# Down projection: the product with the lower left weight block as seven products over both column halves

## The chip, the cores and the metric

The kernel runs on one core of a Trainium2 chip. The metric is the device time of one execution in microseconds, the median of three runs. Most numbers below come from one further execution that the hardware profiler recorded.

## The reference

```
xn = _layernorm(x)                                   # x: 1 x 2048 x 640, float32
a = einsum("bsd,ed->bse", xn, dft_hid_re);  b = einsum("bsd,ed->bse", xn, dft_hid_im)
fnet = einsum("ts,bse->bte", dft_seq_re, a) - einsum("ts,bse->bte", dft_seq_im, b)
gate = einsum("bsd,df->bsf", xn, W_gate);  up = einsum("bsd,df->bsf", xn, W_up)     # f: 1728
h = gate * (gate > 0) * up
out = x + fnet + einsum("bsf,fd->bsd", h, W_down)
```

## The kernel before

**Arithmetic.** A product in float32 is made of three matmuls in the reduced type fp32r (`mm3`, lines 128 to 133): both operands are split (line 124) into a high copy, which ScalarE writes (line 125), and a low part, source minus high copy, which VectorE writes (line 126). The three matmuls are high by high, high by low and low by high.

**Stages.** First the Fourier transform over the sequence, to about 398 us; then gate and up, 26 units of one row block of the hidden layer each, to about 731 us; then the down projection, in which this change lies. It adds three things: the layernorm's transform still to be multiplied by the hidden DFT matrix ("hid", operands in `pqd`), the hidden activations times `W_down` ("f", operands in `hd`), and x itself (`xt`). The output is 640 rows (five row blocks e = 0 to 4 of 128) by 2048 tokens. The tokens are worked in two halves, q = 1 and then q = 0 (`project(q)`, line 1123), and each half is two chunks of 512 columns.

**The seven products.** The contraction blocks of 128 are paired, one "upper" and one "lower". Upper and lower blocks by the two column chunks, and the row blocks 0,1 against 2,3 of the output, make a 2 by 2 block product, and it is done with seven products in place of eight (Strassen's scheme in Winograd's form), named B11, T1, B21, T2, B22, T3 and T4. B11, B12 (used in T1), B21 and B22 are also the names of the four blocks of the moving operand: the first figure says upper (1) or lower (2) contraction blocks, the second says which column chunk. T1 to T4 use sums and differences of them, which VectorE makes. Row block e = 4 is done plainly, as a third column of weights beside B11, T1, B21 and B22. B21 is the product of the lower blocks of the first column chunk with the "lower left" weight block: each of its contraction blocks costs nine matmuls (row blocks 0, 1 and 4, three matmuls each).

**Units.** Each product is made of seven units, numbered 0 to 6: three "hid" units of two, two and one pairs of contraction blocks, an "f" unit of two, the "odd" unit 4 with the left-over rows (short in B21, B22 and T4), and two more "f" units of two. A unit of two blocks has 18 matmuls in B11, T1, B21 and B22 and 12 in T2, T3 and T4. The results gather in PSUM; after the last unit of a product VectorE adds them into an output tile `y` (`add_y`, line 1284) that was loaded with x.

**Order of the work.** All units stand in a list `todo`, in the order B11, T1, B21, T2, the first four units of B22, T3, the rest of B22, T4, for q = 1 and then for q = 0. `drive(4, 2)` walks it: at step i it issues the loads of unit i, prepares unit i-2 (the sums, the high copies on ScalarE, the low parts on VectorE), runs unit i-4 on TensorE and reads what ended with unit i-5. SyncE issues nearly all loads, strictly in this order; VectorE and ScalarE are ordered by a scheduler that a helper `in_turn` keeps near the program's order. Buffers come from pools: `raws` (24 tiles, "rw") for the moving operands as loaded, "ro" for the odd ones, `wraw` (4, "wr") and `wts` (5, "wt") for weights as loaded and as split, `ring2` (3, "cb") for the split moving operand. The weights' sums for T1, T2, T3, T4 and B22 are made once, during gate and up (`pair_weights`, line 1019), and stored to a DRAM array `wparts`.

Of the kernel before, what the change touches and what calls it, by code (L numbers as in the profile page):

```python
# [12 lines left out]
P = 128  # L13
S, D, F = 2048, 640, 1728
KD = D // P
CH = 512
# [41 lines left out]

@with_exitstack
def fnet_reglu_kernel(  # L60
# [40 lines left out]
    wparts = dram_p.tile([P, NPAIR, NW], F32, name="wparts")  # L101
    nc.vector.memset(eps_t, EPS)
# [915 lines left out]

    def pair_weights(k, n):

        t = {}

        def load():
            t["z"] = z = pool("prep").tile([P, Y12 + 2 * P], F32, name="pw")
# [6 lines left out]
        def prepare():  # L1031
# [15 lines left out]
        issues[n + 1].append(lambda: nc.gpsimd.dma_start(wparts[:, k], t["z"][:, :NW]))  # L1047
# [33 lines left out]
    def place(i):  # L1081
        if i % 2 == 0:
            spare[i // 2] = pool("prep").tile([P, Y12 + 2 * P], F32, name="pw")
        return spare[i // 2][:, i % 2 * W2 : (i % 2 + 1) * W2]
# [6 lines left out]
    for k in range(NPAIR):  # L1091
        pair_weights(k, 7 if k == ODD else 13 + k)
# [27 lines left out]
    for n, b, side in (("wraw", 4, "left"), ("ring2", 3, "left"), ("wts", 5, "left"), ("raws", 24, "left"), ("odd", 4, "right"), ("y", 1, "right")):  # L1120
        open_pools[n] = ctx.enter_context(tc.tile_pool(name=n, bufs=b, side=side, reuse_waits="tile"))

    def project(q):
        c0, c1 = 2 * q, 2 * q + 1
        units = [("hid", u) for u in HID_UNITS] + [("f", u) for u in F_UNITS]
        units.insert(ODD_AT, ("odd", (0,)))
        raws, B, y, ends = {}, {}, {}, []

        def get(kind, u):
            what, ks = units[u]  # L1130
# [16 lines left out]
        def unit(name, u, first):  # L1147
            what, ks = units[u]
# [7 lines left out]
            def load():  # L1156
                kind = {"T1": "B12"}.get(name, name)
                if name == "B11" and (q, u) == (1, 0):
                    return
                if kind in ("B11", "B12", "B21"):  # L1160
# [78 lines left out]
            def run():  # L1239
                b, w = t["b"], t["w"]  # L1240
                key, o, row4 = {"B11": ("a", 0, (2 * P, "v1")), "T1": ("b", P, (0, "v2")), "B21": ("c", 0, (2 * P, "v1")),
# [3 lines left out]
                for out, oo, more in [((key, i), o + i * P, more) for i in range(2)] + ([(row4[1], row4[0], name in ("B21", "B22"))] if row4 else []):  # L1245
                    if first and not more:
                        B[out] = bank()
# [118 lines left out]
```

## Time and profile before

| | |
|---|---|
| median of three runs | 1026.95 us (1026.6 to 1027.21) |
| the profiled execution: its span | 1025.6 us |
| PE (TensorE matmul) busy | 1019.3 us, 99%, 4525 matmuls |
| DVE (VectorE) busy | 805.5 us, 79%, 1113 instructions |
| ACT (ScalarE) busy | 448.2 us, 44% |
| moved by DMA | 236.45 MB, 231 GB/s in the mean |
| down projection on PE | 730.9 to 1021.5 us |

The profiled execution's time is its span and what lies around it; here only the span is recorded, 1025.6 us, which is 1.35 us under the median of the timed runs. In the profile's views PE is the matmul part of TensorE and PEld its weight load; `out<-in` names the tiles; "x6" counts instructions; a bracket at a row's end tells how long the engine idled before the row and what it waited for. The granted clock is the share of TensorE's full clock that it was given.

### The profile page before, as it was taken

Reading aid. Unit: us, or ns where it says so; the run is one execution under the profiler, and the core shown is the slowest. Engines: PE = TensorE matmul, PEld = TensorE weight load, DVE = VectorE, ACT = ScalarE, POOL = GpSimd, SP = SyncE. Lnnn points to the kernel's source line nnn. Section 1 sums busy time; section 2 is a strip of 40 time slices with the busy share of each in tenths; the row PEclk is TensorE's granted clock in tenths of the full one; section 3 lists DMA queues with packets and bytes.
Section 4 is the critical chain, followed back from the end, with each engine's and each line's share of the span. In section 5 each row is a group of like instructions: output and inputs, shape, how many; then the busy total and the mean of one; then the engine's idle time right before and its main releaser. Section 6 shows DMA issues by size and latency. Waiting matters only on the chain.

```text
span 1025.6 us, 12560 instructions
## 1 busy us (share of the span) xinstructions
PE 1019.3 (99%) x4525; PEld 843.1 (82%) x4525; DVE 805.5 (79%) x1113; ACT 448.2 (44%) x571; POOL 96.9 (9%) x161
## 2 busy tenths in 40 slices
PE   9999999999999999999999999999999999999998
PEld 7888888888888888888888888888888888888886
DVE  7967976969888797787887888876586779777776
ACT  6664453333334443433335544443454434553442
POOL 2000010121110001421110000000000001000000
PEclk9999999999999999999999999999999999999999
DMA  9884744976869665863474666664595747994655
GB/s 327 321 283 157 264 152 138 338 246 208 350 205 336 228 197 196 265 229 135 172 242 146 224 216 226 236 226 170 198 357 188 254 145 237 385 337 140 218 172 160
DMA packets 104542, 236.45 MB, mean 231 GB/s; under 512 B 11936, under 2 KB 55328, under 8 KB 102944
## 3 DMA queue, kind: packets, MB, share of 16 engines
q1 hardware_dynamic: 86896, 165.49, 47.9%
q0 software_dynamic: 17152, 69.74, 18.9%
q8 instruction: 35, 0.57, 0.2%
q10 hardware_dynamic: 432, 0.43, 0.1%
q14 instruction: 27, 0.22, 0.1%
HBM read 179.50 MB, written 55.07 MB: 229 GB/s over the span
## 4 chain that ended last, share of the span: by engine, by line
PE 97%; DVE 2%; DMA 0%; ACT 0%; issue 0%; SPq 0%; ACTq 0%
PE ps L132 31%; PE ps L131 31%; PE ps L133 31%; PE ps L519 3%; PE ps L548 1%; PE ps L1250 1%; DVE cb L126 1%; DMA raw<-in_dft 0%; DVE raw L686 0%; DVE r L126 0%; DVE sb L561 0%; DVE sa L558 0%; DVE tk L686 0%; ACT cb L125 0%; ACT cb L349 0%
## 5 line engine op out<-in xcount | busy, mean ns | idle before, releaser
L133 PE MATMUL ps<-cb,wt 128*128 128x512 f32 x412 | 160.0, 388 | 0.0
L132 PE MATMUL ps<-cb,wt 128*128 128x512 f32 x412 | 159.9, 388 | 0.0
L131 PE MATMUL ps<-cb,wt 128*128 128x512 f32 x412 | 159.8, 388 | 0.0
L125 ACT ACTIVATE cb<-rw 128x1024 fp32r<-128x1024 f32 x83 | 81.9, 987 | 121.7 <-PE ps L133 105.8
L126 DVE TENSOR_TENSOR cb<-rw,cb 128x1024 fp32r<-128x1024 f32 x83 | 94.0, 1132 | 50.9 <-ACT cb L125 50.5
L125 ACT ACTIVATE cb<-raw 128x1024 fp32r<-128x1024 f32 x64 | 67.8, 1060 | 103.7 <-PE ps L133 94.8
L126 DVE TENSOR_TENSOR cb<-raw,cb 128x1024 fp32r<-128x1024 f32 x64 | 78.2, 1221 | 31.9 <-ACT cb L125 31.6
L131 PE MATMUL ps<-xs_early,gw 128*128 128x512 f32 x260 | 101.1, 389 | 0.0
L132 PE MATMUL ps<-xs_early,gw 128*128 128x512 f32 x260 | 101.1, 389 | 0.0
L133 PE MATMUL ps<-xs_early,gw 128*128 128x512 f32 x260 | 101.1, 389 | 0.0
L133 PEld LDWEIGHTS ps<-cb,wt 128*128 128x128 f32 x412 | 77.3, 188 | 16.1 <-DVE wt L126 0.3
L131 PEld LDWEIGHTS ps<-cb,wt 128*128 128x128 f32 x412 | 77.3, 188 | 16.1
L132 PE MATMUL ps<-cb,xs_late 128*128 128x512 f32 x232 | 90.5, 390 | 0.1
L132 PEld LDWEIGHTS ps<-cb,wt 128*128 128x128 f32 x412 | 77.3, 188 | 15.9
L131 PE MATMUL ps<-cb,xs_late 128*128 128x512 f32 x232 | 90.3, 389 | 0.0
L133 PE MATMUL ps<-cb,xs_late 128*128 128x512 f32 x232 | 90.3, 389 | 0.0
L132 PE MATMUL ps<-cb,xs_early 128*128 128x512 f32 x226 | 87.9, 389 | 0.0
L131 PE MATMUL ps<-cb,xs_early 128*128 128x512 f32 x226 | 87.9, 389 | 0.0
L133 PE MATMUL ps<-cb,xs_early 128*128 128x512 f32 x226 | 87.9, 389 | 0.0
L122 ACT ACTIVATE gw<-z 128x1024 fp32r<-128x1024 f32 (+1 forms) x52 | 56.1, 1109 | 41.3 <-PE ps L133 29.4
L122 ACT ACTIVATE u<-ps 128x512 f32<-128x512 f32 x52 | 31.2, 599 | 89.6 <-PE ps L133 77.8
L867 DVE TENSOR_TENSOR gw<-z,gw 128x1024 fp32r<-128x1024 f32 (+1 forms) x52 | 64.8, 1284 | 2.9 <-ACT gw L122 2.8
(200 smaller groups left out, 1955.8 us busy)
## 6 DMA issues: line engine op xcount, KB each, us to landing
raw<-in_dft SPq DMA_DIRECT2D x94, 512.0 KB, 5.7
wt<-wparts SPq DMA_DIRECT2D x70, 256.0 KB, 3.2
z<-in_wgu SPq DMA_DIRECT2D x26, 640.0 KB, 4.6
hd<-ob POOLq DMA_DIRECT2D x26, 512.0 KB, 3.7
wparts<-pw POOLq DMA_DIRECT2D x12, 1024.0 KB, 4.1
rw<-hd SPq DMA_DIRECT2D x24, 512.0 KB, 5.9
tk<-in_dft SPq DMA_DIRECT2D x16, 512.0 KB, 8.1
rw<-pq SPq DMA_DIRECT2D x16, 512.0 KB, 6.3
```

Source lines behind the costliest of these rows:

```text
L122: return nc.scalar.activation(o, i, AF.Copy)
L125: nc.scalar.activation(hi, src, AF.Copy)
L126: return nc.vector.tensor_tensor(lo, src, hi.bitcast(F32), op=OP.subtract)
L131: nc.tensor.matmul(ps, wh, mh, start=first, stop=False, skip_group_check=more)
L132: nc.tensor.matmul(ps, wh, ml, start=False, stop=False, skip_group_check=more)
L133: nc.tensor.matmul(ps, wl, mh, start=False, stop=last, skip_group_check=more)
L519: nc.tensor.matmul(E[0, key], xn_part(n * SG + j, d)[v == 1], b[:, int(v == 2), j], start=False, stop=n % NH == NH - 1 and (j, v) == (SG - ...
L548: nc.tensor.matmul(E[c, key], xn_part(j, d)[v == 1], b[c][0][:, int(v == 2), j], start=j == 0 and v == 0, stop=False)
L867: tt(self.w[:, 1, cs], self.z[:, cs], self.w[:, 0, cs].bitcast(F32), op=OP.subtract)
L1250: nc.tensor.matmul(B[out], w[:, v, oo : oo + P], b, start=False, stop=u == len(units) - 1 and v == 1, skip_group_check=more)
```

## The change

The product B21 of both token halves, q = 1 and q = 0, has the same weights. Of its contraction blocks the ten full pairs that units 0, 1, 3, 5 and 6 hold are taken out of `project` and done for both halves at once, by a second level of the seven-product scheme (`second_level`): its two column halves are the first chunks of q = 1 (X) and of q = 0 (Y), its two contraction halves are pairs of blocks (QUADS), its two output halves are row blocks 0 and 1. The seven products are named 1, 2, 5, 6, 3, 7 and 4, and each goes over three groups of 2, 2 and 1 pairs of blocks, which makes 21 units. Row block 4 is again done plainly, beside products 1, 2, 5 and 3. Of B21 in `project` only units 2 and 4 (SINGLE) are left.

The operands X and Y are loaded once, by six DMAs into tiles of a new pool `quads` that stay on chip until the end (`fetch`); the output tiles of row blocks 0, 1 and 4 of both first chunks stay on chip too. These loads stand at step 14 of the list (LOADS_AT). The 21 units are put between the others, one after every second step (EVERY) from step 20 on (SINCE), that is from T2 of q = 1 to T1 of q = 0. The sums of weights that they need are made beside the others in `pair_weights` (four sums of 128 columns and a split of 512 for each of five quads) and stored to a new DRAM array `wquads`.

Other things move with it: the moving operands of B21 are still needed for T4, and are now loaded by T3's steps; those of B22's first units are loaded at T1 in place of B21; `raws` has 20 tiles in place of 24; the PSUM banks are named by hand; T4's first two units stand ahead of the left-over units of B21; and the order on TensorE follows the list too. `order` counts 4510 matmuls in place of 4525, and on VectorE 996 and 106 instructions of its two kinds of sums in place of 941 and 96.

```diff
+QUAD_LOW, QUAD_HIGH, NPREP = 16 * P, 20 * P, 24 * P
+QUADS = ((0, 2), (1, 3), (KD, KD + 2), (KD + 1, KD + 3), (KD + 4, KD + 5))
+GROUPS = (("hid", 0, 2, 0), ("f", 0, 2, 2), ("f", 4, 1, 4))
+PREP_ORDER = (0, 2, 1, 3, 4, 5, 7, 6, 8, 9, 10)
...
+        quad = next((i for i, (_, second) in enumerate(QUADS) if second == k), None)
...
+            if quad is not None:
+                halves = [[w[:, Y12 + i * P : Y12 + (i + 1) * P] for i in range(2)] for w in (made[QUADS[quad][0]], z)]
+                (a11, a21), (a12, a22) = halves
+                s1, s2, s3, s4 = (z[:, QUAD_LOW + i * P : QUAD_LOW + (i + 1) * P] for i in range(4))
+                minus = lambda o, i0, i1: nc.vector.scalar_tensor_tensor(o, i0, -1.0, i1, op0=OP.mult, op1=OP.subtract)
+                tt(s1, a22, a21, op=OP.subtract)
+                minus(s2, s1, a11)
+                tt(s3, a11, a21, op=OP.subtract)
+                minus(s4, a12, s2)
+                low = z[:, QUAD_LOW:QUAD_HIGH]
+                split(z[:, QUAD_HIGH:NPREP].bitcast(F32R), low, low)
...
+        def keep():
+            z = t["z"]
+            nc.gpsimd.dma_start(wparts[:, k], z[:, :NW])
+            if quad is not None:
+                for v, at in enumerate((QUAD_HIGH, QUAD_LOW)):
+                    nc.gpsimd.dma_start(wquads[:, quad, :, v], z[:, at : at + 4 * P].rearrange("p (s n) -> p s n", s=4))
...
+    pair_weights(ODD, 7)
+    for i, k in enumerate(PREP_ORDER):
+        pair_weights(k, 13 + i)
...
-    for n, b, side in (("wraw", 4, "left"), ("ring2", 3, "left"), ("wts", 5, "left"), ("raws", 24, "left"), ("odd", 4, "right"), ("y", 1, "right")):
+    for n, b, side in (("wraw", 4, "left"), ("ring2", 3, "left"), ("wts", 5, "left"), ("raws", 20, "left"),
+                       ("odd", 4, "right"), ("y", 1, "right"), ("quads", 1, "right")):
...
+    SINGLE = (2, ODD_AT)
+    LOADS_AT, SINCE, EVERY = 14, 20, 2
+    every = range(len(UNITS))
+    fixed = [bank() for _ in range(8)]
...
+        A, Bk = (fixed[0:2], fixed[2:4]) if q else (fixed[2:4], fixed[0:2])
+        B = {("a", 0): A[0], ("a", 1): A[1], ("b", 0): Bk[0], ("b", 1): Bk[1], ("c", 0): Bk[0], ("c", 1): Bk[1],
+             "v1": fixed[4], "v2": fixed[4], "v3": fixed[4]}
...
+                kind = {"B11": "B11", "T1": "B12", "T3": "B21"}.get(name)
+                if kind:
                     get(kind, u)
-
-                ahead = {("B21", 2): 0, ("B21", 4): 1, ("B21", 6): 2, ("T2", 0): 3, ("T2", 2): 4, ("T2", 3): 5, ("T2", 4): 6}.get((name, u))
+                ahead = {("T1", 2): 0, ("T1", 4): 1, ("T1", 6): 2, ("T2", 0): 3, ("T2", 2): 4, ("T2", 3): 5, ("T2", 4): 6}.get((name, u))
...
+        LOADS_Y = {"B11": ((0, 0), (1, 0), (4, 1), (4, 0)) if q else ((4, 1),), "T1": ((2, 1), (3, 1)), "T2": ((0, 1), (1, 1)), "T4": ((2, 0), (3, 0))}
...
+        steps = []
+        for name, us in (("B11", every), ("T1", every), ("T2", every), ("B22", every[:4]), ("T3", every),
+                         ("B22", every[4:]), ("T4", every[:2]), ("B21", SINGLE), ("T4", every[2:])):
+            whole = SINGLE if name == "B21" else every
...
+    def second_level():
+        X, Y = {}, {}
+        a, x, v = fixed[5:]
+        def fetch(g):
+            what, k, n, _ = GROUPS[g]
+            for t, q in ((X, 1), (Y, 0)):
+                t[g] = o = pool("quads").tile([P, 2 * n, CH], F32, name=f"q{q}{g}")
+                if what == "hid":
+                    nc.sync.dma_start(o, pqd[2 * q][1][:, k : k + 2 * n])
+                else:
+                    first = 2 * k + 1
+                    nc.sync.dma_start(o, hd[q][first : first + 4 * n - 1 : 2, :, :CH].rearrange("f p t -> p f t"))
+        def unit(name, g):
+            what, k, n, at = GROUPS[g]
+            k += KD if what == "f" else 0
+            t = {}
+            halves = slice(0, n), slice(n, 2 * n)
+            part = {"5": 0, "6": 1, "7": 2, "3": 3}.get(name)
+            second = name in ("2", "3", "4")
+            block = {"1": 0, "2": 0, "4": P}.get(name)
+            odd = name in ("1", "2", "5", "3")
+            def load():
+                own = pair(k + n * second, n)[1].rearrange("k p n -> p k n")
+                t["w"] = w = pool("wts").tile([P, 2, 2, 3 * P], F32R, name="wt")[:, :n]
+                if part is not None:
+                    for j in range(n):
+                        nc.sync.dma_start(w[:, j, :, :P].bitcast(F32), wquads[:, at + j, part])
+                if block is not None or odd:
+                    t["r"] = r = pool("wraw").tile([P, 2, 3 * P], F32, name="wr")[:, :n]
+                    if block is not None:
+                        nc.sync.dma_start(r[:, :, :P], own[:, :, block : block + P])
+                    if odd:
+                        nc.sync.dma_start(r[:, :, P : 2 * P], own[:, :, 2 * P : 3 * P])
+            def prepare():
+                lo, hi = halves
+                plus = lambda o, i: nc.vector.tensor_tensor(o, o, i, op=OP.add)
+                with in_turn():
+                    src = {"1": X[g][:, lo], "2": X[g][:, hi], "5": X[g][:, lo], "6": X[g][:, lo], "3": Y[g][:, hi],
+                           "7": Y[g][:, lo], "4": X[g][:, lo]}[name]
+                    if name in "5674":
+                        plus(src, {"5": Y[g][:, lo], "6": Y[g][:, hi], "7": Y[g][:, hi], "4": X[g][:, hi]}[name])
+                    t["b"] = b = pool("ring2").tile([P, 2, SG, CH], F32R, name="cb")[:, :, :n]
+                    lows.append(split(b[:, 0], b[:, 1], src))
+                    if "r" in t:
+                        cs = slice(0 if block is not None else P, 2 * P if odd else P)
+                        split(t["w"][:, :, 0, cs], t["w"][:, :, 1, cs], t["r"][:, :, cs])
+            def run():
+                b, w = t["b"], t["w"]
+                main, fresh = {"1": (a, True), "2": (x, True), "5": (x, True), "6": (a, False), "3": (x, False),
+                               "7": (a, False), "4": (a, False)}[name]
+                for ps, o, new in [(main, 0, fresh)] + ([(v, P, name in ("1", "5"))] if odd else []):
+                    for j in range(n):
+                        mm3(ps, (w[:, j, 0, o : o + P], w[:, j, 1, o : o + P]), (b[:, 0, j], b[:, 1, j]),
+                            new and g == 0 and j == 0, g == len(GROUPS) - 1 and j == n - 1, not new)
+            def read():
+                less = OP.subtract
+                for q, e, ps, op in {"1": ((1, 0, a, OP.add), (0, 4, v, less)), "2": ((1, 0, x, OP.add), (1, 4, v, OP.add)),
+                                     "5": ((0, 1, x, less),), "6": ((0, 0, a, less),), "3": ((0, 0, x, less), (0, 4, v, OP.add)),
+                                     "7": ((0, 1, a, less),), "4": ((1, 1, a, OP.add),)}[name]:
+                    add_y(q, e, 0, ps, op=op)
+            return load, prepare, run, read if g == len(GROUPS) - 1 else idle
...
+        loads = [((lambda g: lambda: fetch(g))(g), idle, idle, idle) for g in range(len(GROUPS))]
+        loads.append((lambda: get_y(0, (0, 0), (1, 0), (4, 0)), idle, idle, idle))
+        return loads, [unit(name, g) for name in "1256374" for g in range(len(GROUPS))]
+    def spread(steps, more, since, every_n):
+        mixed, more = [], list(more)
+        for i, s in enumerate(steps):
+            mixed.append(s)
+            if i >= since and (i - since) % every_n == every_n - 1 and more:
+                mixed.append(more.pop(0))
+        assert not more, len(more)
+        return mixed
+    steps = project(1) + project(0)
+    loads, quads = second_level()
+    steps[LOADS_AT:LOADS_AT] = loads
+    todo.extend(spread(steps, quads, SINCE, EVERY))
+    with tc.manual_schedule(engines={mybir.EngineType.SP, mybir.EngineType.Pool, mybir.EngineType.PE}):
```

Three places where instructions move follow. The names are the tiles with their numbers, so that `rw_6073` is a moving operand, `wr` weights as loaded, `q10` to `q02` the tiles of X (first figure 1) and Y (0), and `y000` an output tile of q = 0.

SyncE's queue of loads before, at T1 of q = 1: the loads of the odd unit 4 and of unit 5 (`rw_5959`).

```order
L1141 DMA ro_5936<-hd1_91 128x512
L1190 DMA wr_5938<-in_wd 128x128
L1191 DMA wr_5938<-wparts_94 128x256
L1145 DMA rw_5959<-hd1_91 128x2x512
L1190 DMA wr_5961<-in_wd 128x2x128
L1191 DMA wr_5961<-wparts_94 128x2x256
```

The same place now: between unit 4's weights and unit 5's operand (`rw_6073`) stand the nine loads of the change.

```order
L1260 DMA wr_5991<-in_wd 128x128
L1261 DMA wr_5991<-wparts_94 128x256
L1384 DMA q10_6012<-pq2_88 128x2048
L1384 DMA q00_6014<-pq0_86 128x2048
L1387 DMA q11_6032<-hd1_91 128x4x512
L1387 DMA q01_6034<-hd0_90 128x4x512
L1387 DMA q12_6054<-hd1_91 128x2x512
L1387 DMA q02_6056<-hd0_90 128x2x512
L1174 DMA y000_6058<-in_xt 128x512
L1174 DMA y100_6060<-in_xt 128x512
L1174 DMA y400_6062<-in_xt 128x512
L1216 DMA rw_6073<-hd1_91 128x2x512
```

Six transfers of four or two blocks of 128 x 512 and three output tiles now stand ahead of unit 5's operand.

VectorE before, near the end, at T4 of q = 0 (from the low part of its unit 2 on):

```order
L126 TENSOR_TENSOR cb_7858<-rw_7191,cb_7858 128x512
L1197 TENSOR_TENSOR ro_7279<-ro_7279,ro_7087 64x512
L1197 TENSOR_TENSOR rw_7304<-rw_7304,rw_7110 128x1024
L126 TENSOR_TENSOR cb_7884<-rw_7221,cb_7884 128x1024
L126 TENSOR_TENSOR wt_7915<-wr_7887,wt_7915 64x256 x2
L1197 TENSOR_TENSOR rw_7325<-rw_7325,rw_7131 128x1024
L1197 TENSOR_TENSOR cb_7912<-ro_7279,cb_7912 64x512
L126 TENSOR_TENSOR cb_7936<-rw_7304,cb_7936 128x1024
L126 TENSOR_TENSOR cb_7940<-rw_7325,cb_7940 128x1024
```

The same place now:

```order
L133 TENSOR_TENSOR cb_8014<-rw_7722,cb_8014 128x512
L1267 TENSOR_TENSOR rw_7786<-rw_7786,rw_7393 128x1024
L1179 TENSOR_TENSOR y000_6058<-ps_5723,y000_6058 128x512
L133 TENSOR_TENSOR cb_8031<-rw_7739,cb_8031 128x1024
L1179 TENSOR_TENSOR y100_6060<-ps_5724,y100_6060 128x512
L1179 TENSOR_TENSOR y400_6062<-ps_5727,y400_6062 128x512
L1267 TENSOR_TENSOR cb_8059<-ro_7766,cb_8059 64x512
L133 TENSOR_TENSOR wt_8062<-wr_8034,wt_8062 64x256 x2
L133 TENSOR_TENSOR cb_8083<-rw_7786,cb_8083 128x1024
L1267 TENSOR_TENSOR rw_7807<-rw_7807,rw_7416 128x1024
L133 TENSOR_TENSOR cb_8087<-rw_7807,cb_8087 128x1024
```

The three reads of the left-over B21 product (`y000`, `y100`, `y400`) have come in between, and the difference for the last unit (`rw_7807`) is made later, after the low part of the unit ahead of it.

More of the change, by code (lines that the diff above doesn't have):

```diff
@@ L1082, in place @@
         if i % 2 == 0:
[L1083 removed]
+            spare[i // 2] = pool("prep").tile([P, NPREP], F32, name="pw")
         return spare[i // 2][:, i % 2 * W2 : (i % 2 + 1) * W2]
@@ new lines, in fnet_reglu_kernel, with get_y, add_y @@
+    missing[0, 3, 0] += 2
+    def get_y(q, *which):
+        for e, c in which:
+            own = f"{q}" if e in (0, 1, 4) and c == 0 else ""
+            y[q, e, c] = t = pool("y").tile([P, CH], F32, name=f"y{e}{c}{own}")
+            nc.sync.dma_start(t, xt[e * P : (e + 1) * P, (2 * q + c) * CH : (2 * q + c + 1) * CH])
+    def add_y(q, e, c, ps, late=False, op=OP.add, at=slice(0, CH), queue=None):
+        t = y[q, e, c][:, at]
+        if op == OP.add:
+            nc.vector.tensor_tensor(t, ps, t, op=OP.add)
+        else:
+            nc.vector.tensor_tensor(t, t, ps, op=op)
+        missing[q, e, c] -= 1
+        if missing[q, e, c] == 0 or queue is not None:
+            first = (2 * q + c) * CH
+            o = out[e * P : (e + 1) * P, first + at.start : first + at.stop]
+            if queue is not None:
+                queue.dma_start(o, t)
+            elif late:
+                nc.sync.dma_start(o, t)
+            else:
+                defer(1, lambda: nc.gpsimd.dma_start(o, t))
```

119 lines of the change are left out of this document (51 added, 68 removed).

## The prediction

> **What bounds the kernel now.** I read the engines' busy times first, then the chain that ended last, then a table by windows of the down projection, and last the timeline of VectorE (DVE) and the DMA queue where the change puts work.
>
> ```profile
> PE 1019.3 (99%) x4525; PEld 843.1 (82%) x4525; DVE 805.5 (79%) x1113; ACT 448.2 (44%) x571; POOL 96.9 (9%) x161
> PE 97%; DVE 2%; DMA 0%; ACT 0%; issue 0%; SPq 0%; ACTq 0%
> 731.00:1021.50 290.50, 290.48 (x1287) 240.30 (x1285) 223.66 (x253) 131.67 (x163) 9.24 (x17) 1.00 0.72 241
> 876.49 0.19 PEld L133 LDWEIGHTS ps<-cb,wt 128*128 128x128 f32 x1 [0.30 <-DVE wt L126]
> ```
>
> TensorE (PE) is busy 99% of the span and carries 97% of the chain. The third row is the down projection (window; busy time and count of PE, PEld, DVE, ACT, POOL; granted clock; DMA share; GB/s): PE has no gap, the granted clock is 1.00. The last row is its only stall worth naming, 0.30 us. So a matmul taken out is gained in full, and every wait put in front of PE is lost in full, as nothing else has slack to give back. VectorE is busy 223.7 of 290.5 us there, 77%.
>
> ```profile
> 794.33 1.36 PE ps L1250 x6
> ```
>
> On the chain six matmuls take 1.36 us, 226.7 ns each.
>
> **The change part by part.** *Matmuls.* Ten blocks of B21 cost 9 matmuls each in two halves, 180. Now five quads cost 3 matmuls in each of 7 products, plus 4 times 3 for row block 4: 5 x 33 = 165. That is 15 fewer, 15 x 226.7 ns = -3.4 us, all on the path. The Trainium skill ("TensorE: Matmul & The Clock Gate", section "Wait — 56ns, not 53.3ns?") prices a matmul of 512 columns at about 216 ns; by it the term would be -3.2 us. The measured row decides.
>
> *Weights' sums in gate and up.* Five of the 26 units get four sums of 128 columns and a split of 512.
>
> ```profile
> 708.76 0.69 DVE L951 TENSOR_TENSOR oa<-ps,u 128x512 f32<-128x512 f32 x1 [1.73 <-PE ps L133]
> 701.26 0.42 DVE L856 TENSOR_TENSOR z<-z 128x256 f32<-128x256 f32 x1
> 701.60 0.28 DVE L857 TENSOR_TENSOR z<-z 128x128 f32<-128x128 f32 x1
> 701.80 0.68 DVE L878 TENSOR_TENSOR ob<-ob,u 128x512 f32<-128x512 f32 x1
> ```
>
> From start to start a 256-wide one takes 0.34 us and a 128-wide one 0.20 us; the split takes 0.605 (below): 4 x 0.20 + 0.605 = 1.4 us. The bracket shows VectorE idle for 1.73 us in such a unit, waiting for PE. I cost this at nothing; without that cover it would be at most 5 x 1.4 = 7 us.
>
> *VectorE's work in the down projection.* It runs its rows back to back where it is dense:
>
> ```profile
> 751.65 1.22 DVE L126 TENSOR_TENSOR cb<-rw,cb 128x1024 fp32r<-128x1024 f32 x1
> 752.79 0.95 DVE L126 TENSOR_TENSOR wt<-wr,wt 128x768 fp32r<-128x768 f32 x1
> 753.66 1.22 DVE L126 TENSOR_TENSOR cb<-rw,cb 128x1024 fp32r<-128x1024 f32 x1
> 754.79 0.69 DVE L1197 TENSOR_TENSOR rw<-rw 128x512 f32<-128x512 f32 x1
> 755.40 0.55 DVE L126 TENSOR_TENSOR wt<-wr,wt 128x384 fp32r<-128x384 f32 x1
> 755.87 0.68 DVE L1284 TENSOR_TENSOR y<-ps,y 128x512 f32<-128x512 f32 x1
> 756.47 0.68 DVE L126 TENSOR_TENSOR cb<-rw,cb 128x512 fp32r<-128x512 f32 x1
> ```
>
> From start to start: 1.135 us for 1024 columns, 0.87 for 768, 0.605 for 512, 0.47 for 384. The 21 new units need 14 low parts of 1024 and 7 of 512 (20.1 us), sums for four products, 8 of 1024 and 4 of 512 (11.5), and the lows of their weights (two products of 2 x 512 + 256, three of 2 x 256 + 128: 5.7), 37.3 us. Twelve more reads of PSUM add 7.3. Gone are ten units of B21, 1.135 + 0.87 each, 20.1. Net +24.5 us: VectorE goes from 223.7 to about 248 of 287 us, 86%. On the mean it fits. What counts is where it doesn't, and where its inputs come late. I find three places.
>
> *Place E, the loads at T1 of q = 1.* The queue of loads now has, ahead of unit 5's operand, six transfers for X and Y (5120 KB), three output tiles (768 KB), two of B22's operands that were loaded with B21 before (1024 KB) and one more output tile (256 KB): 7168 KB, 7.34 MB. Before:
>
> ```profile
> 735.00:757.50 22.50, 22.50 (x101) 18.63 (x100) 17.22 (x21) 11.27 (x15) 0.00 (x0) 1.00 1.01 364
> 740.00:750.00 10.00, 10.00 (x46) 8.28 (x45) 6.33 (x7) 4.52 (x6) 0.00 (x0) 1.00 1.05 390
> 10.00:12.00 2.00, 2.00 (x10) 1.68 (x9) 1.90 (x6) 0.83 (x4) 1.24 (x2) 1.00 1.02 423
> 752.11 0.38 SPq L1145 DMA_DIRECT2D rw<-hd  x1
> rw<-hd SPq DMA_DIRECT2D x1, 512.0 KB, 5.1
> 771.73 0.39 PE L131 MATMUL ps<-cb,wt 128*128 128x512 f32 x1
> 771.96 0.39 PE L132 MATMUL ps<-cb,wt 128*128 128x512 f32 x1
> 772.18 0.39 PE L133 MATMUL ps<-cb,wt 128*128 128x512 f32 x1
> 771.93 1.06 ACT L125 ACTIVATE cb<-rw 128x1024 fp32r<-128x1024 f32 x1 [0.25 <-PE ps L133]
> ```
>
> The first two rows show DMA full (share 1.01 and 1.05) through this stretch, moving 364 to 390 GB/s; the fastest I find elsewhere is 423. Unit 5's operand is issued at 752.11 and lands 5.1 us later, at 757.2, and the queue is full: what is put ahead of it moves it by its own length. At 390 GB/s 7.34 MB take 18.8 us, so it lands at 776.0 (774.6 at 423, 777.4 at 364). Then come the difference (1.135), the high copy (1.06) and the low part (1.135), and after them the second matmul, at 779.3; PE would have come to it at 771.96. That is 7.4 us, and up to 8.0 at the third matmul, whose weights' low part stands behind the operand's on VectorE. Nothing can pass: VectorE, ScalarE and PE each take their rows in order, and behind the waiting difference stand the low parts of units 5 and 6 and of T2. I take +8.0, with bounds 6 (at 423) and 9.4 (at 364); it would be 0 if the landing came by 768.6. The Trainium skill ("DMA: Bandwidth & Descriptors", section "Specifications") gives about 358 GB/s as a core's share of HBM; by it 20.5 us and a wait of 9.7. The window of 390 speaks against so low a limit here.
>
> A pause that long may also cost clock.
>
> ```profile
> 1022.50:1023.50 1.00, 0.00 (x0) 0.00 (x0) 0.00 (x0) 0.00 (x0) 0.00 (x0) 1.00 0.70 216
> 1023.50:1024.50 1.00, 0.00 (x0) 0.00 (x0) 0.00 (x0) 0.00 (x0) 0.00 (x0) 0.98 0.00 0
> 1024.50:1025.60 1.10, 0.00 (x0) 0.00 (x0) 0.00 (x0) 0.00 (x0) 0.00 (x0) 0.50 0.00 0
> 1.06 4.12 PE L113 MATMUL ps<-warm 128*128 128x128 bf16 x47 [1.06 <-DVE warm L109]
> 4.00:6.00 2.00, 1.18 (x22) 1.00 (x18) 1.85 (x8) 1.31 (x4) 0.00 (x0) 1.00 0.90 248
> ```
>
> PE stops at 1021.5, and the granted clock falls to 0.50 at about 1024.46, 3.0 us later. At the start the warm-up matmuls begin at 1.06 and the clock is 1.00 by 4.00, 2.9 us later. So a pause of over 3.0 us would lead to some 3 us of matmuls at half clock, 1.5 us lost; bounds 0 and 1.5, and I take 1.5, since the pause of some 6.7 us before the first of these matmuls is twice as long as it needs. The same page on TensorE (Trainium skill, section "What's actually happening") has a window of 3.4 us for both directions; the rows agree within its granularity.
>
> *Place B, T4 of q = 1.* Its units 0 and 1, the left-over B21 and new units stand close, with reads between them. From unit 1 to unit 5 PE has 82 matmuls, 18.6 us; VectorE has 8 rows of 1024, 13 of 512, 3 of 384, 4 of 256 and 1 of 128: 9.08 + 7.87 + 1.41 + 1.36 + 0.20 = 19.9 us. VectorE enters with a lead of 19 matmuls (4.3 us) less three reads and a low part (2.95), 1.3 us. So 0 is lost if it runs without gaps. It doesn't quite:
>
> ```profile
> 858.65 1.22 DVE L126 TENSOR_TENSOR cb<-rw,cb 128x1024 fp32r<-128x1024 f32 x1
> ...
> 868.27 1.23 DVE L126 TENSOR_TENSOR cb<-rw,cb 128x1024 fp32r<-128x1024 f32 x1
> ```
>
> Between these two starts, in T4 of before, lie 4 rows of 1024, 6 of 512 and 2 of 256: 8.85 us by the paces above, but 9.62 passed, 8.7% more. With that the loss is 1.7. Neither end is nearer, so I take the middle, +0.8.
>
> *Place D, the end.* After the left-over B21's last unit VectorE has on its way to the last unit's operand: a read 0.60, a low part 1.135, two reads 1.2, an odd low 0.6, two weights' lows 0.69, a low 1.135, the difference 1.135, the high copy 1.16, the low 1.135: 8.8 us. PE has 34 matmuls and the first of the last unit, 7.94 us. +0.9, with bounds 0 (if the scheduler's order is made up by lead) and 1.5 (with 8.7% more).
>
> *Sum.* -3.4 + 8.0 + 1.5 + 0.8 + 0.9 = +7.8 us. The profiled span is 1025.6 us, 1.35 us under the median of 1026.95; the difference is put on the median: **1034.7 us**.
>
> **The rivals.** *The pause without the clock.* PE waits as at place E, but the granted clock stays at 1.00, or comes back at once: 1033.2 us.
>
> *The loads are early enough, the short places stay.* SyncE could run further ahead than before, so that the burst starts sooner; only the two T4 places remain: 1026.95 - 3.4 + 0.8 + 0.9 = 1025.3 us. For it speaks that the operand has 768.6 - 757.2 = 11.4 us to spare, in which 4.4 MB pass at 390 GB/s. Against it: 7.34 MB are added, and the share of 1.01 has no room left from 735 on.
>
> *All of it hidden, faster.* One thing decides: whether unit 5's operand of T1 lands by 768.6. That needs the burst issued 7.4 us earlier than I reckon. If it is, and VectorE's leads cover T4, only the matmuls count: 1023.5 us. For it: 86% of VectorE is not full, and before it stalled PE for 0.30 us only. Against it: the same full queue, and the two sums above that end above zero.
>
> **How the numbers follow.** Forecast (pause with clock) 0.40; pause without the clock 0.24; only T4's places 0.20; all hidden 0.16. What a measurement of this kernel can tell from no change is about 0.2%, so "same" is 1024.9 to 1029.0: the third case. Faster 0.16, same 0.20, slower 0.64. The range leaves out the fastest case, and takes in the third: 1025.0; above, 1034.7 + 1.4 (364 GB/s) + 0.9 + 0.6 (places B and D at their upper bounds) = 1037.6, so 1038.0. The two slower cases alone, with place E from 6 to 9.4: 1030 to 1038.
>
> **What would show it.** Right: 4510 matmuls; DMA share near 1.0 without a break from 740 to about 776; a gap of PE of 6 to 8 us at T1's unit 5 of q = 1, near 772, whose wait leads back to the load of `rw` from `hd`; the granted clock at half just after it; small PE stalls by VectorE in T4. Wrong: no gap near 772, or one that another load or VectorE's own backlog ends; a gap in gate and up, which I cost at nothing; or a VectorE that falls behind between T2 and T1 of q = 0, where I find lead enough.

## Result: slower by 1.3%, and the profile after

The changed kernel takes 1040.53 us (median, 1038.6 to 1042.3) against 1026.83 us before; the ratio is 1.0134, interval 1.0119 to 1.0148. The forecast was 1034.7 us, range 1025.0 to 1038.0. The direction and the largest place were right, the size was not: +13.7 us in place of +7.8. The profiled execution took 1038.6 us, the fastest of the four.

The page of the changed kernel, its busy times and the chain that ended last:

```profile
span 1036.8 us, 12735 instructions
PE 1020.4 (98%) x4510; PEld 842.3 (81%) x4510; DVE 837.1 (81%) x1178; ACT 458.5 (44%) x592; POOL 104.7 (10%) x171
PE 91%; DMA 4%; DVE 3%; SPq 1%; issue 0%; ACT 0%; ACTq 0%; DVEq 0%
```

PE has 4510 matmuls as counted, but no longer 97% of the chain: DMA has 4% and VectorE 3%. What PE waits for, by the view of waits (us in total, times, longest):

```profile
PE ps L138 <- ACT wt L132: 7.6, 1, 7.6
PE ps L139 <- DVE cb L133: 3.2, 3, 1.8
...
PE ps L138 <- DVE y L1179: 0.6, 1, 0.6
```

One wait of 7.6 us stands out. The chain around it leads back to the loads:

```profile
753.00 4.88 DMA ro<-hd
...
757.89 3.03 SPq L1387
...
760.97 1.57 SPq L1387
...
764.83 11.61 DMA rw<-hd
...
776.46 1.24 DVE rw L1267
...
777.78 1.06 ACT cb L132
...
780.01 0.96 DVE wt L133
```

This is place E. SyncE is busy issuing the loads of X and Y (L1387), unit 5's operand is issued only at 764.83 and takes 11.6 us in the full queue, so that it lands at 776.44; the forecast was 776.0. Difference, high copy and weights' low part follow, and PE goes on. The same stretch by windows (PE, PEld, DVE, ACT, POOL; granted clock; DMA share; GB/s):

```profile
760.00:770.00 10.00, 10.00 (x45) 8.26 (x44) 5.26 (x7) 2.73 (x4) 0.00 (x0) 1.00 1.02 396
772.00:778.00 6.00, 0.00 (x0) 0.00 (x0) 1.23 (x1) 0.22 (x1) 0.00 (x0) 0.68 1.07 390
780.00:784.00 4.00, 3.92 (x9) 2.72 (x9) 4.00 (x5) 2.65 (x3) 0.00 (x0) 0.50 1.10 358
```

DMA stays full at 390 to 396 GB/s, PE does nothing from 772 to 778, and the granted clock is 0.50 when it starts again: 9 matmuls run in 4 us in place of 17, with a wait of 0.6 us for the weights' low part among them. By the trace's record of the clock it goes to half at 774.16, 2.3 us into PE's wait, and back to 1.00 at 784.40.

Two of the further waits weigh most. The first is in T4 of q = 1 (place B), in the timelines of ScalarE, VectorE and PE, in this order:

```profile
886.39 0.31 ACT L132 ACTIVATE wt<-wr 128x128 fp32r<-128x128 f32 x1 [0.78 <-DMA wr<-in_wd]
886.60 0.62 ACT L129 ACTIVATE cb<-ro 64x512 fp32r<-64x512 f32 x1
889.62 1.06 ACT L132 ACTIVATE cb<-rw 128x1024 fp32r<-128x1024 f32 x1 [1.87 <-DVE rw L1267]
```

```profile
884.26 1.22 DVE L133 TENSOR_TENSOR cb<-q,cb 128x1024 fp32r<-128x1024 f32 x1 [0.21 <-ACT cb L132]
...
890.02 1.22 DVE L1267 TENSOR_TENSOR rw<-rw 128x1024 f32<-128x1024 f32 x1
891.16 1.22 DVE L1414 TENSOR_TENSOR q<-q 128x1024 f32<-128x1024 f32 x1
892.30 2.35 DVE L133 TENSOR_TENSOR cb<-rw,cb 128x1024 fp32r<-128x1024 f32 x2
```

```profile
893.57 0.50 PE L139 MATMUL ps<-cb,wt 128*128 128x512 f32 x1 [1.76 <-DVE cb L133]
```

PE waits 1.9 us (by the distance of its starts) for a low part. ScalarE waits for VectorE's difference ahead of it, and VectorE for nobody: behind 884.26 none of its rows has a bracket. So this wait is VectorE's backlog. The second is in T1 of q = 0, unit 3, 1.1 us at 941.7, where the forecast had nothing. There ScalarE could write the unit's high copy only when PE had done with the buffer:

```profile
938.60 1.06 ACT L132 ACTIVATE cb<-rw 128x1024 fp32r<-128x1024 f32 x1 [1.98 <-PE ps L140]
```

Added up from the starts of PE's matmuls, by what is over 226.7 ns each:

| place | forecast | first profile | second profile (e11_again) |
|---|---|---|---|
| 15 matmuls fewer | -3.4 | -3.4 | -3.4 |
| T1 of q = 1, unit 5, with half clock | 9.5 | 10.4 | 9.3 |
| T4 of q = 1 (B) | 0.8 | 2.0 | 2.4 |
| end (D) | 0.9 | 1.1 | 0.8 |
| T1 of q = 0, unit 3 | 0 | 1.2 | 3.9, of it 1.6 half clock |
| T1 of q = 1, unit 0 (PSUM bank) | 0 | 0.9 | 0.6 |
| span against 1025.6 | +7.8 | +11.2 | +13.7 |

The rows' sums are 12.2 and 13.6; in the first profile the down projection also starts 0.8 us earlier (730.1 in place of 730.9), which leaves 0.2 unassigned. Of the 5.8 us that the forecast lacks against the second profile, T1 of q = 0 has 3.9, place B 1.6 and the PSUM bank 0.6.

### The profile page after: what moved, and what is told of

Read it like the earlier page. It is cut to its first block, busy times and chain, and to the rows that moved or that the text cites. A ratio compares the mean times of both kernels' runs of the same rounds, so it can differ in the third digit from the quotient of the medians.

```text
span 1036.8 us, 12735 instructions
## 1 busy us (share of the span) xinstructions
PE 1020.4 (98%) x4510; PEld 842.3 (81%) x4510; DVE 837.1 (81%) x1178; ACT 458.5 (44%) x592; POOL 104.7 (10%) x171
## 4 chain that ended last, share of the span: by engine, by line
PE 91%; DMA 4%; DVE 3%; SPq 1%; issue 0%; ACT 0%; ACTq 0%; DVEq 0%
PE ps L140 29%; PE ps L139 29%; PE ps L138 29%; PE ps L526 3%; DMA wr<-in_wd 2%; DMA rw<-hd 1%; DVE cb L133 1%; PE ps L555 1%; DVE rw L1267 1%; DMA rw<-pq 1%; PE ps L1318 1%; PE ps L120 1%; DVE wt L133 0%; DMA ro<-hd 0%; SPq L1387 0%
## 5 line engine op out<-in xcount | busy, mean ns | idle before, releaser
L138 PE MATMUL ps<-cb,wt 128*128 128x512 f32 (+1 forms) x407 | 159.1, 391 | 8.3 <-ACT wt L132 7.6
L139 PE MATMUL ps<-cb,wt 128*128 128x512 f32 (+1 forms) x407 | 159.3, 391 | 3.2 <-DVE cb L133 3.2
L140 PE MATMUL ps<-cb,wt 128*128 128x512 f32 (+1 forms) x407 | 158.8, 390 | 0.1
L132 ACT ACTIVATE cb<-rw 128x1024 fp32r<-128x1024 f32 (+1 forms) x73 | 71.1, 976 | 99.2 <-PE ps L140 56.9
L133 DVE TENSOR_TENSOR cb<-rw,cb 128x1024 fp32r<-128x1024 f32 (+1 forms) x73 | 81.5, 1118 | 29.8 <-ACT cb L132 29.5
```

What stands on the lines that cost most here:

```text
L132: nc.scalar.activation(hi, src, AF.Copy)
L133: return nc.vector.tensor_tensor(lo, src, hi.bitcast(F32), op=OP.subtract)
L138: nc.tensor.matmul(ps, wh, mh, start=first, stop=False, skip_group_check=more)
L139: nc.tensor.matmul(ps, wh, ml, start=False, stop=False, skip_group_check=more)
L140: nc.tensor.matmul(ps, wl, mh, start=False, stop=last, skip_group_check=more)
```

## Experiments

**The burst.** `e1_spread` hands the loads out.

```diff
+    WITH = {(1, 'T1', 5): ['X0'], (1, 'T1', 6): ['X1'], (1, 'T2', 1): ['X2'], (1, 'T2', 3): ['y4'], (1, 'T2', 5): ['Y0'], (1, 'B22', 1): ['Y1'], (1, 'B22', 3): ['Y2'], (1, 'T3', 1): ['y0'], (1, 'T3', 3): ['y1']}
...
-    steps[LOADS_AT:LOADS_AT] = loads
```

> The changed kernel, but with the loads of X, Y and the three output tiles handed out one at a time behind nine different units from T1's unit 5 (q = 1) to T3's unit 3, in place of all nine ahead of T1's unit 5. Theory: these loads delay unit 5's operand, and the pause and the slow clock behind it (7.8 us and some 2.6 us more in the profiled execution) go: about 1030 us, 10 less than the changed kernel, and no gap of PE near 772. Rival: VectorE and DMA are overloaded in any case, and the wait only moves to later units: over 1036 us.

Measured 1035.75 us, 4.8 less. PE's waits near 779 are two, of 2.1 and 0.8 us, at unit 6 in place of unit 5: X0 and X1 still stand in a queue that is full to about 776. The clock fell nonetheless and stayed down for 13 matmuls:

```profile
781.00:785.00 4.00, 4.00 (x11) 3.03 (x11) 1.31 (x2) 0.00 (x0) 0.00 (x0) 0.50 0.00 0
```

**The clock.** `e2_clock` fills the pause.

```diff
+                for _ in range(28):
+                    nc.tensor.matmul(fixed[5], t["w"][:, 0, 0, :P], t["b"][:, 0, 0], start=True, stop=True)
...
+            return load, prepare, run_and_wait if (q, name, u) == (1, "T1", 4) else run
```

> The changed kernel with 28 further matmuls behind T1's unit 4 (q = 1), into a PSUM bank that nothing reads, 6.35 us of work inside the pause of 7.8 us: they keep TensorE busy while the operand is awaited. Theory: the pause lets the granted clock fall, and the matmuls behind it lose some 2 us; with the filling, 1038.4 us, and the clock stays at 1.00. Rival: the clock's fall costs nothing on the path (VectorE paces the restart): 1040.5 us, no change.

Measured 1038.61 us, the theory's number. Three of the four executions took 1038.1 to 1038.8 us at a mean clock of 0.999 to 1.000 (the changed kernel's have 0.994 to 0.996), so the long fall is gone there. The profiled one is the fourth, 1041.18 us, and it shows something else. The filling ends at 778.9, PE then waits four times, 2.4 us in all, and the clock falls all the same:

```profile
774.00:778.00 4.00, 4.00 (x19) 3.32 (x18) 0.84 (x1) 0.00 (x0) 0.00 (x0) 1.00 1.06 394
780.00:784.00 4.00, 3.29 (x8) 2.18 (x9) 4.00 (x5) 2.22 (x4) 0.00 (x0) 0.72 1.09 381
```

In that execution the place costs 6.35 us of filling and some 3.8 of waits and half clock, about as much as before the edit. So the pause of 3.0 us, which the prediction read off the end of before, is not needed for a fall.

**A PSUM bank.** `e3_bank`:

```diff
-             "v1": fixed[4], "v2": fixed[4], "v3": fixed[4]}
+             "v1": fixed[7] if q else fixed[4], "v2": fixed[4], "v3": fixed[4]}
```

> As e1_spread, and row block 4 of B11 (q = 1) gathers in a PSUM bank of its own, in place of one shared with T1. Theory: in the changed kernel T1's unit 0 waits 0.9 us for VectorE's reads of that bank (a term the prediction lacked): 0.9 us under e1_spread. Rival: the wait is given back at the next unit that waits for VectorE or a load: the same as e1_spread within 0.3 us.

Measured 1032.79 us, 3.0 under e1_spread, more than either expected. In the profiles the bank's own wait (0.5 us at 759 in e1_spread) is gone. The rest is the clock: the same two waits of 2.1 and 0.8 us stand at 777.3 and 778.7, but 19 matmuls run in the four microseconds behind them in place of 11:

```profile
779.00:783.00 4.00, 4.00 (x19) 3.29 (x18) 2.15 (x3) 0.35 (x1) 0.00 (x0) 1.00 0.00 0
```

So the same waits cost some 2.8 us more in one profile than in the other, and a shift of 1.9 us decided it. The traces' records of the clock show how. In all 18 profiles its changes lie whole multiples of 3.413 us apart; half clock lasts 3.4 us in e2_clock, 6.8 in e1_spread, 10.2 in the changed kernel. In e1_spread:

```profile
776.16:779.57 3.41, 1.47 (x7) 0.84 (x5) 2.12 (x4) 1.79 (x2) 0.00 (x0) 1.00 1.06 321
779.57:786.39 6.82, 6.30 (x16) 4.60 (x15) 3.43 (x5) 0.00 (x0) 0.00 (x0) 0.50 0.05 19
786.39:789.80 3.41, 3.41 (x17) 2.78 (x16) 1.49 (x2) 1.58 (x2) 0.00 (x0) 1.00 0.43 123
```

Carry that spacing through each profile, and reckon the share of each interval that matmuls take, 226.7 ns from each start. Then every interval at full clock with a share below 0.395 ends in a fall, 13 of them ahead of the kernels' last matmuls, and none of the others does. Seven of them, the two nearest to each other in the middle:

| run | interval (us) | share | clock after it |
|---|---|---|---|
| changed kernel | 770.75 to 774.16 | 0.31 | 0.50 |
| e1_spread | 776.16 to 779.57 | 0.35 | 0.50 |
| e5_later | 873.35 to 876.76 | 0.36 | 0.50 |
| e9_ring4 | 872.53 to 875.95 | 0.39 | 0.50 |
| e3_bank | 882.91 to 886.33 | 0.40 | 1.00 |
| changed kernel | 890.22 to 893.63 | 0.41 | 1.00 |
| e3_bank | 773.69 to 777.10 | 0.44 | 1.00 |

So it takes some 2.1 us of waiting within one interval. Place B's wait of 1.9 us lies whole in one and costs no fall; e1_spread's first wait lies whole in one, and e3_bank's, equally long, is parted by the boundary at 777.10. Where the boundaries lie differs from execution to execution.

**Thinning T4.** `e4_thin` is e1_spread with no second-level unit behind the units of T4 and B21 of q = 1.

```diff
-    SINCE, EVERY, SKIP = 16, 2, ()
+    SINCE, EVERY, SKIP = 16, 2, ((1, 'T4'), (1, 'B21'))
```

> As e1_spread, but no unit of the second level stands between T4's units or B21's left-over units of q = 1; the four that stood there come later, up to T2 of q = 0. Theory: VectorE falls behind there (1.9 us lost in the profiled execution): 1.5 to 2 us under e1_spread. Rival: VectorE is short everywhere, and what is moved costs as much in B11 and T1 of q = 0: the same as e1_spread within 0.5 us, or slower.

Measured 1034.58 us, 1.2 less (0.7 between the profiled spans). The wait of 1.9 us at 891 is gone, but 0.7 us at 884 and 0.5 us at 963 are new: the rival has part of it.

**The loads moved out of the full stretch.** `e5_later` is e3_bank with X0, X1 and X2 at T2's units 2, 4 and 6, y4, Y0 and Y1 at B22's units 0, 1 and 3, the rest at T3, and the second level starts ten steps later.

> As e3_bank, but X, Y and the output tiles are loaded from T2's unit 2 (q = 1) on, where the transfers of before leave the DMA engines room (share 0.13 to 0.51 at 780 to 795 us), and the second level's units start five places later (B22's unit 0 or 1). Theory: the 2.9 us of PE's waiting at T1's unit 6 in e3_bank, with the half clock that follows it in some executions, are still these loads' and go: about 1029.8 us, three under e3_bank, the clock at 1.00 throughout; what stays are VectorE's waits (4 to 5 us). Rival: T1 is late for want of VectorE, and the wait stays: 1032.5 us or more.

Measured 1032.8 us, as much as e3_bank. Place E is settled by the rows: PE runs through where it stood still.

```profile
770.00:780.00 10.00, 10.00 (x46) 8.29 (x45) 9.59 (x11) 3.19 (x3) 0.00 (x0) 1.00 0.83 284
780.00:790.00 10.00, 10.00 (x46) 8.28 (x45) 6.51 (x7) 3.46 (x5) 0.00 (x0) 1.00 1.02 358
790.00:800.00 10.00, 8.70 (x39) 6.88 (x38) 7.40 (x9) 5.21 (x6) 0.00 (x0) 1.00 1.06 393
```

But the loads now fill DMA from 780 to 800, and B22's first unit waits 1.5 us for its weights' low part; and T4 of q = 1 now has two waits, of 0.9 and 1.5 us, with a half clock behind them. The expected 1029.8 was wrong by these.

**Is VectorE short?** Two tests: `e6_every3` thins the second level out (EVERY 3), `e7_no_sums` leaves out the sums of X and Y.

```diff
-                    if name in "5674":
+                    if False:
```

> As e5_later, but the second level's units come after every third unit in place of every second, so that they reach to T3 of q = 0. Theory: VectorE's waits come from density (it is 86% busy over the stretch with the second level): thinner, they fall by 1 to 3 us, 1027 to 1029 us. Rival: they come from the short units around T4 and the reads alone, not from density: the same as e5_later within 0.5 us.

> As e5_later, with the sums of X and Y of products 5, 6, 7 and 4 left out (the output is then not the reference's; it is read for time alone): 12 instructions, 11.5 us by the prediction's paces, leave VectorE, nothing else changes. Theory: the waits in T4 of q = 1 and in T1 of q = 0 are VectorE's shortage: 2.5 to 4 us under e5_later. Rival: they come from loads or from the order on SyncE: the same as e5_later within 0.5 us.

Measured 1036.51 and 1033.18 us. Thinner is 3.7 us slower, and some 11 us less of VectorE's work bring nothing. PE's waits without the sums:

```profile
PE ps L139 <- DVE cb L133: 3.2, 4, 1.6
PE ps L1319 <- DVE cb L1268: 2.4, 1, 2.4
PE ps L140 <- DVE wt L133: 1.5, 2, 1.3
```

They still name VectorE. In T4 of q = 1 it isn't its load in this run: it stands idle itself ahead of T4's odd unit, for weights that ScalarE has not split yet, and ScalarE has waited 3.8 us for their load (VectorE's rows, then ScalarE's).

```profile
867.02 0.68 DVE L133 TENSOR_TENSOR cb<-q,cb 128x512 fp32r<-128x512 f32 x1
871.21 0.87 DVE L133 TENSOR_TENSOR wt<-wr,wt 64x256 fp32r<-64x256 f32 x2 [3.51 <-ACT wt L132]
```

```profile
870.76 0.86 ACT L132 ACTIVATE wt<-wr 64x256 fp32r<-64x256 f32 x2 [3.82 <-DMA wr<-in_wd]
```

So this run doesn't clear VectorE in T4, as another wait took the place of its backlog. In T1 of q = 0 1.0 of 2.0 us stay without the sums, and at the end 0.7 of 0.7, which the sums don't reach: VectorE's load alone doesn't explain these.

**The end.** `e8_end` moves the left-over units of B21 of q = 0 ahead of B22's last units, with `("c", 0)`, `("c", 1)` and `"v3"` in the banks 5, 6 and 7.

> As e5_later, but the left-over units of B21 of q = 0 stand behind T3 in place of between T4's units, in the PSUM banks that the second level no longer uses then. Theory: place D, the two waits of together 1.4 us near the end, comes from the reads and the odd unit that stand between T4's units: 1.0 to 1.4 us under e5_later. Rival: T4 ends as late for its last operand's difference, high copy and low part alone: the same as e5_later within 0.3 us.

Measured 1034.2 us, 1.4 more than e5_later, with executions from 1032.4 to 1037.3. In the profile the end's wait is gone, one of 1.1 us at 1002.8 is new. Neither theory holds; the place is not the cause.

**Reach.** What is left is how far ahead an operand may be prepared: three buffers of `ring2`. Two tests on e5_later, each paid for with two of `raws`:

```diff
-    for n, b, side in (("wraw", 4, "left"), ("ring2", 3, "left"), ("wts", 5, "left"), ("raws", 20, "left"),
... e9_ring4:
+    for n, b, side in (("wraw", 4, "left"), ("ring2", 4, "left"), ("wts", 5, "left"), ("raws", 18, "left"),
... e10_wts6:
+    for n, b, side in (("wraw", 4, "left"), ("ring2", 3, "left"), ("wts", 6, "left"), ("raws", 18, "left"),
```

> As e5_later, but with four buffers in place of three for the split moving operand (ring2), paid for with 18 in place of 20 buffers of raws. Theory: leaving out VectorE's sums changed nothing, so the waits between short units (3 to 12 matmuls) come from reach: ScalarE may write the operand of a unit only when the unit three places before it is done, and short units leave 2 to 4 us for high copy, low part and what stands between. With one place more the waits of T4 of q = 1, T1 of q = 0 and the end shrink: 1.5 to 3 us under e5_later. Rival: the weights' loads, which reach SyncE's queue late, set the waits: the same as e5_later within 0.5 us, or slower for the fewer raws.

> As e5_later, but with six buffers in place of five for the split weights (wts) and 18 of raws. Theory (reach of the operand): the same as e5_later within 0.5 us. Rival: SyncE stands at a weight load until one of five buffers is free, and what is queued behind it (the odd unit's weights in T4, which landed 4.5 us after their issue) comes late: 1 to 2.5 us under e5_later.

e9_ring4: 1027.24 us, 5.6 less. e10_wts6: 1035.89 us, 3.1 more. The operand's buffer it is, and not the weights' (its 18 raws, or the sixth buffer, even cost something). In e9_ring4's profile the waits in T1 of q = 0 and at the end are gone; 1.6 us at 798 and, in T4 of q = 1, 0.5 and 1.5 us with a fall stay. ScalarE's waits for PE in the down projection, in e5_later, in e9_ring4 and in the kernel before:

```profile
ACT cb L132 <- PE ps L140: 82.2, 51, 4.3
```

```profile
ACT cb L132 <- PE ps L140: 58.4, 38, 4.1
```

```profile
ACT cb L125 <- PE ps L133: 115.6, 62, 3.4
```

51 operands waited until PE had freed a buffer, 38 with a fourth one. The count alone proves nothing: before has 62, and PE lost nothing by them, as its units are longer. It fits that less of VectorE's work brought nothing, and that PE's waits stand beside units of 3 to 12 matmuls: three such units last 2 to 8 us, with high copy, low part and what stands between to be done in them.

**The changed kernel again.** `e11_again`, unaltered.

> The changed kernel once more, unaltered. Its first profiled execution had a span of 1036.8 us, 1038.15 with the 1.35 us that lie around it in before, under all but one of its timed runs (1038.6 to 1042.3). Theory: executions of it differ by 2 us and more, for the pause at T1's unit 5 ends with a transfer and the clock comes back at a time of its own; the second profile differs in these two. Rival: timed runs are always some 2 us above the profiled one: the profile shows 1036.8 again, the median 1040.5.

Median 1040.88 us; its profile has a span of 1039.3 us in place of 1036.8. The pauses are the same within 0.5 us at unit 5, but at T1 of q = 0 the clock fell once more, behind a wait of 1.8 us:

```profile
943.00:947.00 4.00, 4.00 (x11) 3.12 (x11) 4.00 (x6) 2.40 (x3) 0.00 (x0) 0.57 0.42 156
```

This execution took 1041.09 us, 0.2 above the median, and the first profile's was the fastest of its four. The two profiles differ by a clock fall and the wait ahead of it.

**Both together.** `e12_best` is e9_ring4 with T4 of q = 1 free of second-level units.

> As e9_ring4, and no unit of the second level stands between T4's units or B21's left-over units of q = 1. By the theory of reach (short units beside short units): 1 us under e9_ring4, about 1029 us; with every wait gone it would be 1023.5. Rival: the units only carry the wait with them: the same as e9_ring4 within 0.5 us.

Measured 1029.09 us, 1.9 more. The second level reaches further into q = 0, and waits of together 1.9 us stand near 990 to 995; the one of 1.6 us at 798 stays.

**One buffer alone, and on before.** `e13_after_ring4` and `e14_before_ring4` have four buffers of ring2 in the changed kernel (raws 18) and in the kernel before (raws 24, as it was).

> The changed kernel with its burst of loads, but with four buffers of the split operand (and 18 of raws), the edit of e9_ring4 alone. Theory (reach is a cause of its own): the waits in T4 of q = 1, in T1 of q = 0 and at the end go as they did there, 4 to 5.6 us under the changed kernel, 1035 to 1036.7 us; the pause at T1's unit 5 stays. Rival: the burst's pause hides what the buffer brings: within 1 us of the changed kernel.

> The kernel before with four buffers of the split operand and nothing else changed. Theory: its units have 9 matmuls or more nearly everywhere and PE waits for 0.3 us only, so reach costs it nothing: the same time within 0.5 us. Rival: the buffer makes any version faster: 1 us or more under before.

e13: 1036.78 us, 3.8 to 4.1 under the changed kernel; the pause stays at 7.3 us, the waits in T1 of q = 0 and at the end are gone. Reach is a cause of its own. e14: 1034.73 us, 7.5 slower than before, which neither theory expected. All of it is one place, the stage's start:

```profile
731.00:741.00 10.00, 4.43 (x20) 3.35 (x19) 2.20 (x4) 2.58 (x4) 0.53 (x1) 0.86 0.61 186
741.00:745.00 4.00, 4.00 (x9) 2.84 (x10) 2.76 (x4) 2.57 (x4) 0.00 (x0) 0.50 1.05 389
```

PE waits 5.7 us for the first loaded weights of B11, and the clock falls; behind 745 no wait over 0.15 us follows. So the buffer does not make before faster. In the trace SyncE stands at the stage's second load (L1143) until 735.3, at last for the end of gate and up's matmuls; that the larger pools lie over tiles still in use there is likely, and wasn't tried.

**Loads and early weights.** `e15_loads` is e9_ring4 with X at T2's units 0, 1 and 3 and Y at T3's units 0, 2 and 4; `e16_early` has besides T4's odd weights of q = 1 loaded with T4's unit 1.

> As e9_ring4, with X loaded from T2's unit 0 and Y from T3's unit 0 on, so that none of them stands just ahead of the weights of B22's first units. Theory: e9_ring4's wait of 1.6 us at 798 us (DMA share 1.07 from 790 to 800) was these loads' work: 1 to 1.7 us under e9_ring4, about 1025.8 us. Rival: VectorE's reads of T2 set that wait, or X's earlier loads bring back a wait in T1: 1027.2 us or more.

> As e15_loads, with the weights of T4's odd unit (q = 1) loaded three units earlier, into a buffer of their own. Theory: in e9_ring4 they landed 4.5 us after an issue that came late on SyncE, and PE's waits of together 2.1 us near 875, with the half clock behind them, follow from that: 1.5 to 3.5 us under e15_loads, 1023 to 1024.5 us, faster than before. Rival: VectorE, busy 9.4 of 10 us there, sets them: the same as e15_loads within 0.5 us.

e15_loads: 1025.5 us; its ratio to before is 0.9988, interval 0.9978 to 0.9997, the one version clear of before. e16_early: 1026.28 us, no gain. PE's waits in e15_loads:

```profile
PE ps L139 <- DVE cb L133: 1.2, 1, 1.2
...
PE ps L140 <- DVE wt L133: 0.3, 1, 0.3
```

The wait of 1.6 us at 798 has shrunk to 0.5, that in T4 stays, and nothing else: span 1023.5 us. T4's wait is not the odd weights' lateness, as e16_early has it too, 1.3 us. What PE waits for in e16_early is VectorE, whose rows stand without a bracket from 862 on, busy for 11.57 of 11.70 us:

```profile
862.00:873.70 11.70, 10.63 (x47) 8.44 (x45) 11.57 (x16) 5.48 (x8) 1.08 (x2) 1.00 0.83 246
```

So VectorE's backlog in T4, place B, is the largest of the waits that are left.

## Why the prediction was wrong, point by point

*Matmuls.* Right: 4510, -3.4 us. With some 2 us of waits left, e15_loads has a span 2.1 us under before's.

*Weights' sums in gate and up at nothing.* Right as far as the profiles tell: the down projection starts at 730.1 and 730.9 us in the changed kernel's two, at 730.9 before.

*Place E.* Right in place and cause, and nearly in size: landing 776.44 against 776.0; pause and clock 10.4 and 9.3 against 9.5. What the sum took as a queue at 390 GB/s ran at 390 to 396. The rate of 358 GB/s that the Trainium skill states ("DMA: Bandwidth & Descriptors", section "Specifications") is passed in these rows. SyncE's time for issuing the big loads (9.6 us from 755.2 to 764.8) stands ahead of the landing too; the sum left it out, and it adds nothing while DMA is full (1.02 from 760 to 770). e5_later shows that without the loads there the pause is gone.

*The clock.* Right that it falls, wrong in the rule "a pause of over 3.0 us", which was read off one pause. In the changed kernel itself it fell 2.3 us into the wait, and in other runs behind waits of 2.0 to 2.4 us in all (e9_ring4, e11_again, e2_clock). What decides in these profiles is how little of an interval of 3.413 us matmuls take. That the term for place E came out near (1.5 us, against 2.1 and 1.5 in the two profiles) is luck in part, and the sum allowed for one fall at one place, where executions have one or two. The Trainium skill ("TensorE: Matmul & The Clock Gate", section "What's actually happening") has a window of some 3.4 us that runs freely, and a fall after an idle one; the intervals agree with the window, but falls came behind intervals that matmuls took up to 0.39 of.

*Places B and D, and "lead enough" elsewhere: the step that failed.* The prediction found lead enough for VectorE between T2 and T1 of q = 0, and put T1 of q = 0 at nothing; it cost 1.2 us in one profile and, with a fall, 3.9 in the other. The test was VectorE's busy time against PE's, and that time was well foreseen (246.8 us from 731 to 1031, against 248). The test was not enough: units of 3 to 12 matmuls put between the others shorten the time that three operand buffers span, and ScalarE can't write ahead. A fourth buffer takes these waits away (e13_after_ring4, and 5.6 us in e9_ring4). The prediction never priced the buffer. Weights' loads that reach ScalarE late have a part in T1 of q = 0 too; no run separates it.

At place B the mechanism was right and the size wrong: VectorE's backlog, 2.0 and 2.4 us. The prediction's own sum with rows 8.7% slower gave 1.7; it took the middle between that and 0, 0.8. Place D came out as summed, 1.1 and 0.8 against 0.9, though it too goes with a fourth buffer.

*PSUM bank.* Overlooked: v1 and v2 share one bank, 0.6 to 0.9 us in the profiles.

*The measured sum.* 1040.5 to e5_later's 1032.8: 7.7 us for the loads, with a bank and the later start in it. To e9_ring4's 1027.2: 5.6 for reach. To e15_loads' 1025.5: 1.7 for the loads' new place. Against 1023.5, the forecast's case in which all is hidden, 2.0 us stay.

## What to carry to other kernels

Price a burst of loads by the queue that it meets: where the DMA share is 1.0, each megabyte delays all that is behind it by its own length (7.34 MB moved a landing from 757.2 to 776.4 us here), so keep operands on chip only where their one load can go into a stretch with room.

When short units are put between long ones, count the buffers ahead of the engine in units' time, not the helpers' busy time: three units of 18 matmuls are 12 us, of 3 to 12 matmuls 2 to 8, and a helper at 86% that may not start is late all the same. Where its rows do stand without a gap, as VectorE's in T4, take the upper end of the sum.

## What was not expected of the hardware

The granted clock changed only at multiples of 3.413 us, and fell behind every such interval of which matmuls took less than 0.395; each fall cost 1.5 to 2.8 us. It fell behind waits of 2.0 us in all (e9_ring4) and not behind 2.9 us (e3_bank). Part of the spread from run to run goes with the clock: in e9_ring4 eight executions with a mean clock of 1.000 take 1026.4 to 1027.3 us, three with 0.998 take 1028.6 to 1029.3. Versions with such waits spread by 1 to 5 us (e8_end 1032.4 to 1037.3), before by under 2.
